# Attention, token mixing and a two-pass MLP on one core: plain products in the first pass, DVE adds the weights' words, input sums made ahead

## The chip, the core and the metric

The kernel runs on one core of a Trainium2 chip. The metric is the device time of one execution in microseconds (us); of several executions the median is given. TensorE is PE in the profile, VectorE DVE, ScalarE ACT, GpSimd POOL and SyncE, which issues the DMAs, SP.

## What is computed

```python
scores = scale * np.matmul(q, k.transpose(0, 1, 3, 2)) - np.log(S)      # B, H, S, D = 4, 12, 448, 64
x = (1.0 / (1.0 + np.exp(-scores))) @ v                                 # heads side by side: (4, 448, 768)
u = x + (x.transpose(0, 2, 1) @ U @ V).transpose(0, 2, 1)               # U, V of rank 32
x = u + np.maximum(u @ w_ch1, 0.0) @ w_ch2                              # 768 -> 3072 -> 768
theta = x @ w_theta
y = einsum('ts,bsd->btd', w_tok_r, x * cos(theta)) + einsum('ts,bsd->btd', w_tok_i, x * sin(theta))
u = x + y
out = u + np.maximum(u @ w_ch, 0.0)
```

The inputs q, k, v are float32; the weights arrive as float64, and the kernel puts their two 32-bit words together itself.

## The kernel before

After the attention the activations lie in SBUF, 768 channels as six strips of 128 partitions, two batches (896 columns) to a tensor: `XC` holds batches 0 and 1, a second tensor batches 2 and 3, which go to DRAM as `xb_d`. Every matmul of the MLP runs in float32 by three products: each operand is split in a high part (ScalarE copies it to the PE's type) and a low part (the rest, a subtraction on DVE, `lo_dve` L128, or on POOL, `lo_pool`, through L119).

**Two passes.** The MLP runs over batches 0 and 1 first and over 2 and 3 after that, each in `NB` = 12 blocks of 256 hidden columns; u = 0..11 is the first pass, u = 12..23 the second. Between them, in the turn, `XC` is swapped with `xb_d` through DRAM (L1123, L1124). A block has two stages. `ch1(u)` multiplies the activations with the block's w1 and applies ReLU; `ch2(u)` multiplies the result `g` with w2 in six parts of twelve matmuls each (L786 to L788), and after each part DVE adds the PSUM bank to `XC` (L790). There are two such banks (`ps_y`), so part m waits for the addition of part m - 2. A period is `ch1(u)` with `ch2(u - 1)`: part 0 of it ahead of `ch1`'s sixth step, parts 1 to 5 behind `ch1`.

**Plain or seven products.** A block's `ch1` is a 2x2 product of halves: two batches by two halves of hidden columns, each summed over two halves of the channels. `ch1_plain` makes it with 8 half products, 72 matmuls. `ch1_step` makes it with 7 (`STEPS`), 63 matmuls, from sums of weight blocks (S1 to S4, made in place by DVE in `w1_sums`, L277 to L280) and of inputs (T1, T2, T3 and a new B12, made by `t_chain` and `t_first`), and puts the four outputs together from PSUM banks and copies: `partial` (a copy `c` on ScalarE, L755), `whole` (DVE adds a bank to it, L759), `split_c` and `split_bank` (ReLU and split). Blocks below `PLAIN` = 2 are plain.

**Conversions.** In the first pass each period converts the weights of a later block, four tiles of 128x768: `Conv.size` loads the next tile and takes the Abs of the high words on ScalarE (L159), `sign` puts sign and mantissa together (DVE, L163 and L164), `low` scales the low words (DVE, L169 and L174), and `fin` in `keep` adds the two (POOL, L122) and stores the result in `w_d` in DRAM, from where the second pass loads it again. In the second pass the periods have two conversions each of what the last stage needs (`kept_jobs`: `tok0` to `tok6`, `wc0` to `wc5`, `th0` to `th5`); a `tok` tile is then transposed by PE (L356), and all of them go through one buffer, `sp`.

**What sets the order.** The order of every engine's instructions is written by hand: `period(u)` returns two hooks, `after_c(n)`, called behind the n-th step of `ch1`, and `after_y(m)`, called behind part m of `ch2`, and what they issue stands on its engine's queue at that place. `take` starts the next kept conversion with its Abs, `kstep` does its next step. At the turn, `turn_forms` swaps `XC`, loads and splits the inputs of the second pass and makes their sums.

Of the kernel before, what the change touches and what calls it, by code (L numbers as in the profile page):

```python
# [24 lines left out]
def tile_kernel(  # L25
# [551 lines left out]
    queue_w("w1", 2, 0)  # L577
    queue_w("w1", 2, 1)
    queue_w("w2", 1, 1)
    for u in range(2, NB):  # L580
# [289 lines left out]
    def part(t, d):  # L870
        return XC[:, d, t * S:(t + 1) * S]

    def chain(kk, los):
        return t_chain(kk, part(0, kk), part(1, kk), part(0, H3 + kk), part(1, H3 + kk), los)

    for t in range(2):
        for j in range(2):
            for h in range(2):
                ch1_plain(1, t, j, h)
            if (t, j) == (0, 0):  # L880
                w_jobs["w1", 2, 1].step()
                w_jobs["w1", 2, 0].step()
            if (t, j) == (0, 1):
                blocks(1, 0)
                plain_out(1, 0)
                w_jobs["w1", 2, 0].step()
                w_jobs["w1", 2, 0].step()
# [528 lines left out]
```

## Time and profile before

| | |
|---|---|
| median of 3 executions | 1378.13 us (1375.36 to 1379.81) |
| the profiled execution: its time, its span | 1383.18 us, 1381.4 us |
| granted PE clock over the span, as a share of 2.4 GHz | 0.934 |
| busy: PE, DVE, ACT, POOL | 1208.0, 876.0, 537.9, 574.2 us |

The span is what the profiler saw from the first to the last instruction; the execution's own time has what lies around it too. Busy times of the engines lie beside each other, so they don't add up to the span, and a share of it is an average over stages: attention up to about 200 us, the first pass up to about 676, the second up to about 1086, the last stage behind it. What bounds a stage is read from the stage's own window and from what PE waits for in it.

### The profile page before, as it was taken

What the parts mean: (1) busy time and instruction counts of PE and PEld (TensorE: products, weight loads), DVE (VectorE), ACT (ScalarE), POOL (GpSimd) and SP (SyncE); (2) the same over time, 40 slices, a digit from 0 to 9 for tenths busy, and PEclk for the clock granted to TensorE, in tenths of its full rate; (3) what the DMA queues carried; (4) which work ended last, traced back from release to release, by engine and by line L of the source; (5) the groups of instructions that cost most, each with busy time, mean ns of one, the idle gap of its engine ahead of it and who ended that gap; (6) DMA issues with size and microseconds to landing.
All of it is one profiled execution on the core that took longest, in us unless ns stands there. A gap on an engine that the chain in (4) does not pass through costs nothing.

```text
span 1381.4 us, 16213 instructions
## 1 busy us (share of the span) xinstructions
PE 1208.0 (87%) x6022; PEld 1016.9 (74%) x6022; DVE 876.0 (63%) x1061; ACT 537.9 (39%) x856; POOL 574.2 (42%) x399
## 2 busy tenths in 40 slices
PE   8899998487888887777587779989989999999998
PEld 4444457377777777676477778878879999999997
DVE  5677756688888898856445556677764464372443
ACT  6667762233333333322343334434434253261110
POOL 1121212366666666756344447755555042230000
PEclk9999999699888899999789999999999999999999
DMA  8677723144444334333542333444322600030244
GB/s 138 140 150 162 167 76 109 34 137 137 137 137 138 122 119 132 118 113 106 193 116 77 95 109 114 160 156 151 138 92 70 241 1 0 1 122 17 30 65 67
DMA packets 213279, 151.44 MB, mean 110 GB/s; under 512 B 160464, under 2 KB 194384, under 8 KB 213072
## 3 DMA queue, kind: packets, MB, share of 16 engines
q1 hardware_dynamic: 187216, 146.96, 36.1%
q10 hardware_dynamic: 25984, 3.44, 1.8%
q8 instruction: 47, 0.77, 0.2%
q14 instruction: 32, 0.26, 0.1%
HBM read 107.84 MB, written 42.53 MB: 109 GB/s over the span
## 4 chain that ended last, share of the span: by engine, by line
PE 44%; DVE 17%; issue 9%; POOL 9%; ACT 3%; DMA 1%; SPq 0%; POOLq 0%; DVEq 0%; ACTq 0%
PE ac L704 5%; PE y L786 5%; PE y L787 4%; PE y L788 4%; DVE ca_w L164 3%; POOL f_A L119 3%; PE y L1299 3%; PE y L1298 3%; PE y L1297 3%; PE bd L704 2%; DVE ws_w L163 2%; PE th L1221 2%; PE th L1224 2%; PE th L1222 2%; DVE XC L790 2%
## 5 line engine op out<-in xcount | busy, mean ns | idle before, releaser
L786 PE MATMUL y<-g,w 128*128 128x448 f32 x552 | 223.7, 405 | 121.9 <-DVE XC L790 121.8
L786 PEld LDWEIGHTS y<-g,w 128*128 128x128 f32 x552 | 114.7, 208 | 146.1 <-DVE XC L790 136.1
L790 DVE TENSOR_TENSOR XC<-y,XC 128x896 f32<-128x896 f32 x144 | 155.9, 1084 | 97.8 <-PE y L788 97.7
L787 PE MATMUL y<-g,w 128*128 128x448 f32 x552 | 217.3, 394 | 0.0
L788 PE MATMUL y<-g,w 128*128 128x448 f32 x552 | 216.0, 391 | 0.0
L122 POOL TENSOR_TENSOR ca_w<-ca_w,ws_w 128x768 f32<-128x768 f32 x48 | 93.9, 1956 | 170.2 <-DVE ws_w L174 160.6
L769 POOL TENSOR_TENSOR g<-c,g 128x448 fp32r<-128x448 f32 x66 | 89.6, 1361 | 98.3 <-ACT g L116 94.8
L788 PEld LDWEIGHTS y<-g,w 128*128 128x128 f32 x552 | 114.2, 207 | 10.8
L787 PEld LDWEIGHTS y<-g,w 128*128 128x128 f32 x552 | 115.0, 208 | 9.7
L491 ACT ACTIVATE A<-sc,bias_s 112x896 f32<-112x896 f32 x96 | 91.5, 1005 | 23.6 <-PE sc L487 23.5
L704 PE MATMUL ac<-u_T,f_S 128*128 128x448 f32 x396 | 90.2, 373 | 9.4 <-ACT c L755 9.4
L119 POOL TENSOR_TENSOR zl<-t,zh 128x768 fp32r<-128x768 f32 x23 | 42.7, 1880 | 129.5 <-ACT zh L116 129.5
L767 ACT ACTIVATE c<-c 128x448 f32<-128x448 f32 x66 | 37.7, 572 | 136.1 <-DVE c L759 136.1
L704 PEld LDWEIGHTS ac<-u_T,f_S 128*128 128x128 f32 x396 | 75.9, 192 | 16.7 <-ACT c L755 10.1
L755 ACT ACTIVATE c<-ac 128x448 f32<-128x448 f32 x66 | 35.9, 544 | 131.7 <-PE ac L704 126.0
L500 PE MATMUL av<-A,v 112*64 112x448 f32 x384 | 85.6, 569 | 1.0 <-ACT XO L116 1.0
L164 DVE SCALAR_TENSOR_TENSOR ca_w<-ca_w,ws_w 128x768 uint32<-128x768 uint32 x48 | 77.4, 1613 | 3.1
L119 POOL TENSOR_TENSOR f_S<-r,f_S 128x384 fp32r<-128x384 f32 x48 | 59.4, 1248 | 38.0 <-ACT f_S L116 37.9
L119 POOL TENSOR_TENSOR w<-ca_w,w 128x768 fp32r<-128x768 f32 x23 | 52.1, 2266 | 28.8 <-ACT w L116 26.6
L163 DVE TENSOR_SCALAR ws_w<-ws_w 128x768 uint32<-128x768 uint32 x48 | 60.7, 1264 | 4.4 <-POOL f L119 2.7
L1297 PE MATMUL y<-tok,zh 128*128 128x448 f32 x168 | 62.0, 369 | 0.0
L1298 PE MATMUL y<-tok,zh 128*128 128x448 f32 x168 | 61.7, 368 | 0.0
(225 smaller groups left out, 2699.7 us busy)
## 6 DMA issues: line engine op xcount, KB each, us to landing
ws_w<-in_moe_w_ch_dram SPq DMA_DIRECT2D x48, 768.0 KB, 5.0
w_d<-ca_w SPq DMA_DIRECT2D x48, 384.0 KB, 2.8
r<-w_d SPq DMA_DIRECT2D x24, 384.0 KB, 4.8
r<-w_d SPq DMA_DIRECT2D x12, 768.0 KB, 7.1
k<-in_k_dram SPq DMA_DIRECT2D x96, 56.0 KB, 2.9
q<-in_q_dram SPq DMA_DIRECT2D x92, 56.0 KB, 2.4
v<-in_v_dram SPq DMA_DIRECT2D x44, 112.0 KB, 2.9
ws_wc<-in_moe_w_ch_dram SPq DMA_DIRECT2D x6, 768.0 KB, 5.8
```

The lines of the kernel that those rows point to most:

```text
L119: nc.gpsimd.tensor_sub(o, a, b)
L122: nc.gpsimd.tensor_add(o, a, b)
L164: nc.vector.scalar_tensor_tensor(out=A, in0=A, scalar=3, in1=hw, op0=ALU.logical_shift_left, op1=ALU.bitwise_or)
L491: nc.scalar.activation(a, ps[:CP, :, :S], AF.Sigmoid, bias=bias_s[:CP], scale=SCALE)
L704: nc.tensor.matmul(o, l, r, start=first and kk == 0 and n == 0, stop=last and kk == H3 - 1 and n == 2, skip_group_check=more,)
L769: eng.tensor_sub(g[:, 1].bitcast(F32R), c, g[:, 0])
L786: nc.tensor.matmul(o, wh, gh, start=j == 0, stop=False)
L787: nc.tensor.matmul(o, wh, gl, start=False, stop=False)
L788: nc.tensor.matmul(o, wl, gh, start=False, stop=j == FB - 1)
L790: nc.vector.tensor_add(x, ps[:, :, :S], x)
L1297: nc.tensor.matmul(o, zh[:, sl], tok_h[:, i, :], start=n == 0, stop=False)
L1298: nc.tensor.matmul(o, zh[:, sl], tok_l[:, i, :], start=False, stop=False)
```

## The change

All twelve blocks of the first pass are plain (`PLAIN = NB`), with a hook of their own, `plain_period`; `period` serves the second pass alone. The addition of the two words goes from POOL to DVE: in the first pass from block 1 on (`adder`), and for `tok` and `wc` tiles. The T sums of the first pass go; those of the second pass are made during blocks 3 to 8 of the first (`sums_ahead`), from `xb_d`, with the new B12 kept in DRAM (`t4_d`), so that `turn_forms` only loads and splits. In the second pass the low parts of S1 to S4 go from POOL to DVE, and the steps of the kept conversions stand at other places.

```diff
-    wd_t, A_w = {}, {}
+    wd_t, A_w, adder = {}, {}, [nc.gpsimd]
...
         def fin(a, e):
-            add_pool(a, a, e)
+            adder[0].tensor_add(a, a, e)
...
     def conv_kept(name, src, kk, turns):
-            split(st["o"].bitcast(F32R), a, e, nc.vector if turns else nc.gpsimd)
+            split(st["o"].bitcast(F32R), a, e, nc.vector)
...
     def conv_tok(i):
-            add_pool(st["n"], a, e)
+            nc.vector.tensor_add(st["n"], a, e)
...
-    PLAIN = 2
+    PLAIN = NB
...
+    def sums_ahead(kk):
+        ts = [temp(f"ts{kk}_{n}") for n in range(3)]
+        b12, b22, b11 = ts
+        nc.sync.dma_start(out=b22, in_=xb_d[:, H3 + kk, S:])
+        nc.sync.dma_start(out=b12, in_=xb_d[:, kk, S:])
+        nc.sync.dma_start(out=b11, in_=xb_d[:, kk, :S])
+        def second():
+            nc.vector.tensor_sub(b22, b22, b12)
+            t_split("T3", kk, b22, lo_pool)
+            nc.vector.tensor_sub(b12, b12, b11)
+            t_split("T1", kk, b12, lo_pool)
+        def third():
+            nc.vector.tensor_add(b22, b22, b11)
+            t_split("T2", kk, b22, lo_pool)
+            b21 = temp(f"ts{kk}_3")
+            nc.sync.dma_start(out=b21, in_=xb_d[:, H3 + kk, :S])
+            ts.append(b21)
+        def fourth():
+            nc.vector.tensor_sub(ts[3], ts[3], b22)
+            nc.sync.dma_start(out=t4_d[:, kk], in_=ts[3])
+        return [second, third, fourth]
...
+    adder[0] = nc.vector
...
-    ends = [chain(kk, (lo_dve, lo_pool, lo_dve)) for kk in range(2)]
...
+    def plain_period(u):
+        a, b = (w_jobs["w1", u + 1, j] if more else None for j in range(2))
+        c, d = (w_jobs["w2", u, j] for j in range(2))
...
+        def after_c(n):
+            if n == 0:
+                if not more:
+                    load_w1(0)
+                step(a)
+                if two:
+                    w2_high(u - 1, 1, u - 1)
+                    w2_low(u - 1, 1, u - 1)
+                step(b)
...
+            if n == 7 and more:
+                for j in range(2):
+                    w1_plain(u + 1, j, u + 1, True)
...
+            if n == 7 and not more:
+                load_u(lo_in("B22"), xb_d[:, H3:, S:])
+                load_u(lo_in("B12"), t4_d)
...
+        def after_y(s):
...
+            if s == 1:
+                if more:
+                    w1_low(u + 1)
+                if two:
+                    step(d, 2)
+                    w2_high(u, 0, u)
+                    w2_low(u, 0, u)
...
+            if s == 3:
+                blocks(u, 1)
+                plain_out(u, 1)
+                if not more:
+                    w1_sums(0)
+                    w1_split(0, NB, "S3", "S2", "S1", "S4")
+                    w2_high(u, 1, u, True)
+                    w2_low(u, 1, u)
...
     def period(u):
         def after_c(n):
             if n == 0:
                 partial(u, 0, 0)
...
-                if second:
-                    take(kA)
+                kstep(kB)
+                kstep(kA)
...
         def after_y(s):
...
-                forms("S3")
-                kstep(kB)
...
+            if s == 2:
+                if nxt is not None:
+                    w1_sums(i + 1)
+                forms("S3", "S2", lo=lo_dve)
+            if s == 3:
+                forms("S1", "S4", lo=lo_dve)
...
+    for u in range(1, NB):
+        after_c, after_y = plain_period(u)
+        for n, (t, j, h) in enumerate(halves):
+            ch1_plain(u, t, j, h)
+            after_c(n)
+        ch2(u - 1, after_y)
...
     def turn_forms(s):
-        if s < 3:
-            t_chain(
+        if s == 0:
+            split_b("B22", lo_dve)
+            load_w1(1)
...
     kept_jobs[0].load()
+    take(kA)
     ch1(NB, after_c)
```

Three places of the engines' order follow. In the names, `y_4_1_1` is part 1 of block 4's `ch2` for batch 1, and `ws_w2_5_1` and `ca_w2_5_1` are the words of a conversion.

DVE in the first pass, before, while PE works on `ch2(4)` behind `ch1(5)`:

```order
L790 TENSOR_TENSOR XC_67<-y_4_1_1_3633,XC_67 128x2x448
L277 TENSOR_TENSOR ca_w1_6_1_3504<-ca_w1_6_1_3504 128x384
L278 TENSOR_TENSOR ca_w1_6_1_3504<-ca_w1_6_0_3488,ca_w1_6_1_3504 128x384
L279 TENSOR_TENSOR ca_w1_6_0_3488<-ca_w1_6_1_3504,ca_w1_6_0_3488 128x384
L280 TENSOR_TENSOR ca_w1_6_0_3488<-ca_w1_6_0_3488 128x384
L163 TENSOR_SCALAR ws_w2_5_1_3502<-ws_w2_5_1_3502 128x768
L164 SCALAR_TENSOR_TENSOR ca_w2_5_1_3609<-ca_w2_5_1_3609,ws_w2_5_1_3502 128x768
L790 TENSOR_TENSOR XC_67<-y_4_1_2_3655,XC_67 128x2x448
L169 TENSOR_SCALAR ws_w2_5_1_3502<-ca_w2_5_1_3609 128x768
L174 SCALAR_TENSOR_TENSOR ws_w2_5_1_3502<-ws_w2_5_1_3502 128x768
L790 TENSOR_TENSOR XC_67<-y_4_0_0_3676,XC_67 128x2x448
```

The same place in the change:

```order
L795 TENSOR_TENSOR XC_67<-y_4_0_0_3535,XC_67 128x2x448
L163 TENSOR_SCALAR ws_w2_5_1_3425<-ws_w2_5_1_3425 128x768
L164 SCALAR_TENSOR_TENSOR ca_w2_5_1_3501<-ca_w2_5_1_3501,ws_w2_5_1_3425 128x768
L795 TENSOR_TENSOR XC_67<-y_4_0_1_3551,XC_67 128x2x448
L169 TENSOR_SCALAR ws_w2_5_1_3425<-ca_w2_5_1_3501 128x768
L174 SCALAR_TENSOR_TENSOR ws_w2_5_1_3425<-ws_w2_5_1_3425 128x768
L216 TENSOR_TENSOR ca_w2_5_1_3501<-ca_w2_5_1_3501,ws_w2_5_1_3425 128x768
L795 TENSOR_TENSOR XC_67<-y_4_0_2_3576,XC_67 128x2x448
L795 TENSOR_TENSOR XC_67<-y_4_1_0_3596,XC_67 128x2x448
L718 SCALAR_TENSOR_TENSOR g_5_10_3610<-bc_5_3478,g_5_10_3610 128x448
```

The sums of weights ahead of the conversion are gone, the addition L216 stands behind L174, and all six additions to `XC` (now L795) are in this stretch and what follows it.

ScalarE at the turn, before:

```order
L116 ACTIVATE u_B22_2289<-u_B22_2289 128x1344
L116 ACTIVATE w2_12_1_5351<-r2_0_5105 128x768
L755 ACTIVATE c_12_00_5368<-ac_12_5358 128x448
L159 ACTIVATE ca_tok0_5372<-ws_tok0_5356 112x512
L755 ACTIVATE c_12_01_5395<-ac_12_5358 128x448
L755 ACTIVATE c_12_11_5421<-ac_12_5358 128x448
L767 ACTIVATE c_12_11_5421<-c_12_11_5421 128x448
```

In the change:

```order
L116 ACTIVATE u_B12_2289<-u_B12_2289 128x1344
L116 ACTIVATE w2_12_1_5173<-r2_0_4940 128x768
L159 ACTIVATE ca_tok0_5182<-ws_tok0_5178 112x512
L760 ACTIVATE c_12_00_5194<-ac_12_5184 128x448
L760 ACTIVATE c_12_01_5219<-ac_12_5184 128x448
L760 ACTIVATE c_12_11_5243<-ac_12_5184 128x448
L772 ACTIVATE c_12_11_5243<-c_12_11_5243 128x448
```

The Abs of `tok0` stood behind the first copy of `ch1(12)` and now stands ahead of it.

DVE in the second pass, during `ch2(13)`, before:

```order
L790 TENSOR_TENSOR XC_67<-y_13_1_1_5874,XC_67 128x2x448
L277 TENSOR_TENSOR r1_3_1_5749<-r1_3_1_5749 128x384
L278 TENSOR_TENSOR r1_3_1_5749<-r1_3_0_5747,r1_3_1_5749 128x384
L279 TENSOR_TENSOR r1_3_0_5747<-r1_3_1_5749,r1_3_0_5747 128x384
L280 TENSOR_TENSOR r1_3_0_5747<-r1_3_0_5747 128x384
L163 TENSOR_SCALAR ws_tok4_5754<-ws_tok4_5754 112x512
L164 SCALAR_TENSOR_TENSOR ca_tok4_5850<-ca_tok4_5850,ws_tok4_5754 112x512
L790 TENSOR_TENSOR XC_67<-y_13_1_2_5896,XC_67 128x2x448
L169 TENSOR_SCALAR ws_tok4_5754<-ca_tok4_5850 112x512
L174 SCALAR_TENSOR_TENSOR ws_tok4_5754<-ws_tok4_5754 112x512
L790 TENSOR_TENSOR XC_67<-y_13_0_0_5917,XC_67 128x2x448
L759 TENSOR_TENSOR c_14_01_5781<-bd_14_5758,c_14_01_5781 128x448
```

In the change:

```order
L795 TENSOR_TENSOR XC_67<-y_13_1_1_5699,XC_67 128x2x448
L795 TENSOR_TENSOR XC_67<-y_13_1_2_5714,XC_67 128x2x448
L284 TENSOR_TENSOR r1_3_1_5577<-r1_3_1_5577 128x384
L285 TENSOR_TENSOR r1_3_1_5577<-r1_3_0_5575,r1_3_1_5577 128x384
L286 TENSOR_TENSOR r1_3_0_5575<-r1_3_1_5577,r1_3_0_5575 128x384
L287 TENSOR_TENSOR r1_3_0_5575<-r1_3_0_5575 128x384
L128 TENSOR_TENSOR f_15_S3_5687<-r1_3_1_5577,f_15_S3_5687 128x384
L128 TENSOR_TENSOR f_15_S2_5688<-r1_3_0_5575,f_15_S2_5688 128x384
L795 TENSOR_TENSOR XC_67<-y_13_0_0_5736,XC_67 128x2x448
L128 TENSOR_TENSOR f_15_S1_5690<-r1_3_1_5577,f_15_S1_5690 128x384
L128 TENSOR_TENSOR f_15_S4_5691<-r1_3_0_5575,f_15_S4_5691 128x384
L764 TENSOR_TENSOR c_14_01_5605<-bd_14_5582,c_14_01_5605 128x448
```

Here the low parts of S1 to S4 (`f_15_S3` and the others) come in behind the sums, and the conversion's operations L163 to L174 that stood between the additions to `XC` are gone from this stretch.

## Rows read from the trace of the kernel before

**Rows 1.** The page, parts 1 and 2: busy time; 40 slices.

```profile
PE 1208.0 (87%) x6022; PEld 1016.9 (74%) x6022; DVE 876.0 (63%) x1061; ACT 537.9 (39%) x856; POOL 574.2 (42%) x399
...
PEclk9999999699888899999789999999999999999999
```

**Rows 2.** Waits of PE, 225 to 1071 us: waited for, us, times, longest.

```profile
PE y L786 <- DVE XC L790: 121.8, 29, 14.9
PE tkt L356 <- POOL sp_tok L122: 14.6, 3, 4.9
```

**Rows 3.** Windows by stage: length, busy us (x) by engine, clock, DMA, GB/s.

```profile
234.66:275.03 40.37, 19.45 (x74) 16.95 (x72) 26.66 (x38) 11.26 (x21) 12.43 (x11) 0.70 0.17 54
422.92:460.25 37.33, 30.89 (x137) 27.61 (x136) 30.74 (x30) 13.47 (x23) 25.06 (x18) 0.86 0.41 127
643.84:702.75 58.91, 38.29 (x137) 31.95 (x137) 27.46 (x32) 17.51 (x29) 21.07 (x17) 0.75 0.41 132
702.75:745.10 42.35, 33.06 (x144) 29.17 (x144) 22.35 (x28) 15.34 (x30) 24.28 (x21) 0.88 0.30 89
783.13:820.88 37.75, 30.79 (x145) 27.71 (x144) 20.30 (x24) 12.21 (x23) 18.09 (x14) 0.91 0.32 98
983.34:1016.12 32.78, 28.52 (x136) 25.04 (x135) 25.30 (x28) 14.56 (x26) 16.02 (x13) 1.00 0.32 121
1016.12:1043.48 27.36, 27.36 (x136) 25.35 (x135) 14.89 (x17) 11.15 (x21) 15.50 (x14) 1.00 0.31 116
```

**Rows 4.** Timeline of DVE: start, us, operation, idle before and releaser.

```profile
408.96 0.56 DVE L277 TENSOR_TENSOR ca_w<-ca_w 128x384 f32<-128x384 f32 x1 [3.36 <-POOL f_A L119]
...
414.17 1.08 DVE L790 TENSOR_TENSOR XC<-y,XC 128x896 f32<-128x896 f32 x1
```

**Rows 5.** Timeline of PE, at three of its waits.

```profile
415.30 0.74 PE L786 MATMUL y<-g,w 128*128 128x448 f32 x1 [6.91 <-DVE XC L790]
...
770.44 0.47 PE L786 MATMUL y<-g,w 128*128 128x448 f32 x1 [2.14 <-DVE XC L790]
...
778.00 1.01 PE L356 MATMUL tkt<-ident,sp_tok 112*128 112x112 f32 x4 [4.86 <-POOL sp_tok L122]
```

**Rows 6.** DVE and POOL by line, 422.92 to 460.25 us: busy, mean ns.

```profile
L164 DVE SCALAR_TENSOR_TENSOR ca_w<-ca_w,ws_w 128x768 uint32<-128x768 uint32 x4 | 6.8, 1710 | 0.3
L163 DVE TENSOR_SCALAR ws_w<-ws_w 128x768 uint32<-128x768 uint32 x4 | 6.6, 1645 | 0.0
...
L174 DVE SCALAR_TENSOR_TENSOR ws_w<-ws_w 128x768 f32<-128x768 uint32 x4 | 4.5, 1129 | 0.1
L169 DVE TENSOR_SCALAR ws_w<-ca_w 128x768 uint32<-128x768 uint32 x4 | 2.8, 704 | 0.0
...
L122 POOL TENSOR_TENSOR ca_w<-ca_w,ws_w 128x768 f32<-128x768 f32 x5 | 9.7, 1939 | 6.3 <-DVE ws_w L174 6.3
```

**Rows 7.** Lines of DVE over the whole run: count, duration ns shortest/median/longest.

```profile
L163 DVE TENSOR_SCALAR ws_w<-ws_w x48: 549/1359/2216, 19.1 to 629.7; 128x768 uint32<-128x768 uint32 x48
...
L164 DVE SCALAR_TENSOR_TENSOR ca_w<-ca_w,ws_w x48: 957/1634/2455, 19.7 to 631.1; 128x768 uint32<-128x768 uint32 x48
...
L169 DVE TENSOR_SCALAR ws_w<-ca_w x48: 543/556/2179, 23.5 to 633.7; 128x768 uint32<-128x768 uint32 x48
...
L174 DVE SCALAR_TENSOR_TENSOR ws_w<-ws_w x48: 958/960/2492, 24.1 to 634.9; 128x768 f32<-128x768 uint32 x48
...
L187 DVE TENSOR_TENSOR ca_th<-ca_th,sp_th x6: 958/1138/1326, 928.9 to 1016.8; 128x768 f32<-128x768 f32 x6
...
L790 DVE TENSOR_TENSOR XC<-y,XC x144: 1074/1082/1093, 253.5 to 1085.6; 128x896 f32<-128x896 f32 x144
```

**Rows 8.** Timelines of DVE, ScalarE and PE in the turn.

```profile
676.76 1.09 DVE L790 TENSOR_TENSOR XC<-y,XC 128x896 f32<-128x896 f32 x1 [1.26 <-PE y L788]
...
692.54 0.66 ACT L159 ACTIVATE ca_tok<-ws_tok 112x512 f32<-112x512 f32 x1 [13.12 <-DMA ws_tok<-in_moe_w_tok_r_dram]
...
693.68 3.73 PE L704 MATMUL ac<-u_T,f_S 128*128 128x448 f32 x9 [9.44 <-ACT c L755]
```

More of the change, by code (lines that the diff above doesn't have):

```diff
@@ L262, in w1_plain, with w1_low @@
             hi_act(t[:, 0], a)
-            lo_pool(t[:, 1], a, t[:, 0])
             w1_t[u, j, h] = t
+            if not later:
+                lo_pool(t[:, 1], a, t[:, 0])
+    def w1_low(u):
+        for j in range(2):
+            for h in range(2):
+                t = w1_t[u, j, h]
+                lo_pool(t[:, 1], w1_block(u, j, h), t[:, 0])
     USE = ("A11", "S3", "S2", "A12", "S1", "S4", "A22")
@@ L576, in tile_kernel @@
     queue_w("w1", 1, 1)
[L577 to L580, printed above, removed]
+    for u in range(1, NB):
         if u + 1 < NB:
@@ L866, in tile_kernel @@
         u_tile(uf2, n)
-    w_jobs["w1", 2, 0].step()
     late["sp"], sp_st = pool("sp")
[L870 to L887, printed above, removed]
-            if (t, j) == (1, 0):
-                w_jobs["w1", 2, 1].step()
-                w_jobs["w2", 1, 1].step()
-                ends = [chain(kk, (lo_dve, lo_pool, lo_dve)) for kk in range(2)]
-    for end in ends:
-        end()
-    chain(2, (lo_dve, lo_pool, lo_dve))()
-    for kk in range(H3):
-        t_first(kk, part(0, kk), part(1, kk), lo_pool if kk == 1 else lo_dve)
-    def y_first(s):
-        if s == 0:
-            w_jobs["w1", 2, 1].step()
-            w_jobs["w1", 2, 1].step()
-        if s == 1:
-            w1_forms(2)
-            w1_split(2, 2, "A11", "A12", "A22")
-        if s == 2:
-            w1_sums(2)
-            w1_split(2, 2, "S3", "S2", lo=lo_dve)
-            w_jobs["w2", 1, 1].step()
-        if s == 3:
-            blocks(1, 1)
-            plain_out(1, 1)
-            w1_split(2, 2, "S1")
-        if s == 4:
-            w1_split(2, 2, "S4")
-            w_jobs["w2", 1, 1].step()
-        if s == 5:
-            w_jobs["w2", 1, 1].step()
-            w_jobs["w1", 3, 0].step()
-    ch2(0, y_first)
     kq = list(kept_jobs)
@@ L946, in period, with forms @@
+    ahead = []
+    def period(u):
+        i = u % NB
         lone, last = u == NB, u == NU - 1
-        def step(j):
-            if j is not None:
-                j.step()
-        def forms(*names):
+        nxt = None if last else u + 1
+        def forms(*names, lo=lo_pool):
             if nxt is not None:
-                w1_split((i + 1) % NB, nxt, *names)
+                w1_split(i + 1, nxt, *names, lo=lo)
         def after_c(n):
@@ L1056, in after_y @@
                 kstep(kB)
-                kstep(kB)
-                if not second and i + 2 < NB:
-                    w_jobs["w1", i + 2, 0].step()
+                if u < NU - 2:
+                    take(kA)
                 if u == NU - 2:
                     load_w2(i + 1)
-                if i == NB - 1 and not last:
-                    w2_high(i, 1, u, True)
-                    w2_low(i, 1, u)
         return after_c, after_y
@@ L1129, in tile_kernel @@
     kept_jobs[0].load()
+    take(kA)
     ch1(NB, after_c)
```

184 lines of the change are left out of this document (84 added, 100 removed).

## The prediction

> **What bounds the kernel now.** I read the page first. TensorE (PE) is busy for 1208 of 1381.4 us, and its granted clock stands at 0.8 or 0.9 over much of the middle of the span and at 0.6 in one slice [rows 1]: PE is the bound only where it doesn't wait. So the next view is PE's waits in the two passes. Two entries hold nearly all of them: 121.8 us in 29 waits for VectorE's (DVE's) `XC` addition of L790, which frees one of the two `y` banks, and 14.6 us in three waits for GpSimd's (POOL's) addition in a `tok` conversion, L122 [rows 2].
>
> The windows by stage say what each is worth [rows 3]. The last of them is the measure: 27.36 us for 135 matmuls (the row counts one of a neighbour) with PE busy throughout, at the full 2.4 GHz (granted clock 1.00), so 0.2027 us for each. A first-pass period of the same 135 matmuls takes 37.33 us, with DVE busy for 30.74, POOL for 25.06 and a clock of 0.86. Those ten microseconds over the floor are what the change is about.
>
> The timelines show how such a wait arises. The sums of the next block (L277) wait 3.36 us for POOL, which has the conversion's addition ahead of their operands; the conversion queued behind the sums follows, and only then the `XC` addition, 5.2 us after L277 began [rows 4]. Meanwhile PE stands for 6.91 us. Its first matmul after this takes 0.74 us, the first after a wait of 2.14 us only 0.47 [rows 5], and the granted clock of windows with long waits is 0.70 to 0.88 [rows 3]. A short wait costs itself; a long one costs the half clock (1.2 GHz) after it too.
>
> POOL also slows DVE. In that window the four operations of a conversion take 1.645, 1.710, 0.704 and 1.129 us [rows 6], 5.19 together; at their shortest they take 0.549, 0.957, 0.543 and 0.958, 3.01 together [rows 7]. Four conversions thus lose 8.7 us beside 25.06 us of POOL work: 0.35 us per us of POOL.
>
> **The change, part by part.** All against the profiled execution of 1383.18 us, which is 5.05 us (0.4%) over the median of the three runs.
>
> 1. `ch2(0)`, 234.66 to 275.03, takes 40.37 us with PE busy for 19.45 [rows 3]. DVE makes the T sums and the first sums of weights there; both go. What is left is 72 matmuls, 72 x 0.2027 = 14.6, and half a microsecond of waits: 15.1. **Minus 25.3.** Ends: 14.6 and, with one wait of the size in [rows 5] for the conversions in it, 22.
>
> 2. Ten periods of the first pass, 275.03 to 643.84, 368.8 us [rows 3]. Plain blocks have 72 products' matmuls instead of 63, so the floor rises from 27.36 to 144 x 0.2027 = 29.19 us: 18.3 us are paid in ten periods. Against this DVE and POOL lose their chain: no sums, no `c` partials, and the conversion's addition runs on DVE right behind the operation that feeds it. DVE's load without POOL beside it is four conversions of 3.01 plus an addition of 0.96 (DVE's L187, 128x768, at its shortest [rows 7]), 15.9; six `XC` additions of 1.08, 6.5; four ReLU differences, estimated at 0.6 by their 448 columns, 2.4; in six periods the sums made ahead, some 1.2. That is 24.8 to 26.0. The POOL work left beside it is four low parts of half a block, estimated at half of a 1.94 us operation [rows 6] each, two of about 2.0 and one or two for the T forms, 8 to 10 us; at 0.35 it adds 3.2. DVE then needs 28 to 29.2 us, PE 29.2. Two engines so nearly equal, with two `y` banks between them, don't meet without waits: the additions of parts 3 to 5 stand behind the fourth conversion, as the order listing of DVE shows. I take 2 us of waits per period, short ones that keep the full clock: 31.2. The lower end is 29.3 (no waits), the upper 35.1 (each microsecond of POOL delays DVE by a whole one, 26 + 9). The last period has no conversion for a next block: 29.6. Together 9 x 31.2 + 29.6 = 310.4. **Minus 58.4.** The loads that the sums made ahead issue on SP's queue (four per strip, plus a store) are hidden as long as they are issued a part before their use; without that cover DVE would wait for each, some microseconds in six periods, which the upper end holds.
>
> 3. The turn, 643.84 to 702.75, 58.91 us [rows 3]. `ch2(11)` becomes 14.6 of matmuls and some 5 of waiting for the last weights' low parts, which POOL makes behind four others: 19.6. What follows it doesn't go: the swap of `XC` with DRAM and the load of `ws_tok` behind it in SP's queue. From the last `XC` addition (676.76) to the Abs of `tok0` (692.54) it takes 15.8 us, and PE waits 9.44 of them [rows 8]. The change puts this Abs ahead of `partial(12,0,0)` on ScalarE (the order listing shows it), so PE stops after two products where it had done four. After the Abs (0.66) and the copy (0.5) five products of nine matmuls remain, 9.1, and the half clock after such a wait costs about 3.6 (the three products after it took 9.07 us to 702.75, 5.5 at full clock). 19.6 + 0.3 + 15.8 + 1.2 + 9.1 + 3.6 = 49.6. **Minus 9.3.** Ends: minus 15 and nothing.
>
> 4. Second pass, `ch1(13)` to `ch1(22)`, 702.75 to 1016.12, nine periods in 313.4 us [rows 3]. Its matmuls stay, 9 x 27.36 = 246.2. The `tok` addition goes to DVE, behind its own source, so the 4.86 us before each of three transposes [rows 2, 5] go; four low parts per period move from POOL to DVE behind the sums that they read. I add the six transposes (1.0 us each, [rows 5]) and remaining waits. A `tok` period now has 10.4 us over the floor, of which 4.9 is the wait and 2 the transposes; of the other 3.5 I leave 1.5. Of the 5.4 of a `th` period (983.34) I leave 2.0, of a `wc` period, which has neither, 1.2. Three periods of each: 14.1; and 4 for the first, which starts at a low clock. 246.2 + 6 + 14.1 + 4 = 270.3. **Minus 43.1.** Ends: minus 25 and minus 55.
>
> What lies before 234.66 and after 1043.48 keeps its work; I count nothing. The sum is minus 25.3, 58.4, 9.3 and 43.1, or 136.1: 1247.1 for that execution, and less 5.05 **1242 us** on the median's scale.
>
> [...] The same window shows the operations of two SBUF inputs and those of one grow beside POOL, while `XC` additions, whose one input is in PSUM, take 1.074 to 1.093 us in all 144 cases [rows 7]. [...]
>
> **The rivals.**
> A. DVE is the bound of the first pass: 35.1 per period. For it: the adds have two SBUF inputs, and L174 has been as long as 2.49 us [rows 7]. Against: 0.35. It costs 9 x 3.9 = 35: 1277.
> B. The second pass gains nothing, since its waits are replaced: DVE gets the low parts and the `tok` additions ahead of its `XC` additions (the order listing of DVE in `ch2(13)`). Against: DVE was busy for 20.3 of 37.75 us there, POOL for 18.1 [rows 3]. 1242 + 43 = 1285.
> C. Slower: every conversion runs at its longest, 2.22 + 2.46 + 2.18 + 2.49 and 1.33 for the addition [rows 7], 10.7. Four take 43, and with the 10 of additions and ReLU a period takes 53. The mechanism is DVE's queue in the first pass alone, and it decides from 31.2 + 136/9 = 46.3 us per period on; at 47 the time is 1242 + 142 = 1384. Against it stand the medians, far nearer the shortest.
> D. PE is never kept waiting: 29.3 per period (17 less), and the second pass at its lower end (12 less): 1213.
> That the change doesn't do what it says is excluded by the order listings.
>
> **How the numbers follow.** Forecast 0.68, A 0.14, B 0.09, C 0.05, D 0.04. The predicted time is the forecast's, 1242. The range from 1210 to 1290 takes in D, A and B and the ends of the terms 3 and 4; A and B together, and C, lie outside. A measurement of this kernel tells 0.3% (4 us) from no change. Only C, and little else, ends above 1378: faster 0.95, the same 0.01, slower 0.04.
>
> **What would show it.** Right: PE's windows between starts of `ch1` of 29.3 to 33 us in the first pass with 144 matmuls and a clock near 1.00; a wait of PE for `XC` additions under 40 us in all; no wait of transposes for POOL; 15 us for `ch2(0)`; a wait of about 13 us in the turn for ScalarE's copy behind `ca_tok`. Wrong: conversions' operations on DVE still above 4.5 us per four (A), second-pass periods near 35 us (B), first-pass DVE busy throughout at over 35 us (A, C).

## The result, and the profile after

The changed kernel takes 1292.88 us (median of 4 runs, 1290.99 to 1295.45) against 1377.41 us before: a ratio of 0.939, 95% interval 0.936 to 0.941, or 84.5 us less. Forecast were 1242 us with a range from 1210 to 1290, so the direction was right and the size was not: the time lies 51 us above the forecast and 3 us outside its range.

The profiled execution took 1295.45 us (span 1293.7). The page answers to [rows 1] so:

```profile
PE 1198.7 (93%) x6112; PEld 1010.9 (78%) x6112; DVE 870.8 (67%) x1102; ACT 483.5 (37%) x752; POOL 328.7 (25%) x232
...
PEclk9989999999999999987899999989999999999999
```

POOL lost 245 us of work, DVE almost none, and PE's granted clock is 0.971 over the span and lowest around the turn (0.77 in the turn's window). PE's waits from 190 to 1000 us, as in [rows 2] (waited for: us in total, times, longest):

```profile
PE ac L709 <- ACT c L760: 34.2, 12, 15.8
PE y L791 <- DVE XC L795: 23.5, 31, 1.7
PE tkt L363 <- DVE XC L795: 8.3, 3, 2.8
PE bd L709 <- DVE c L764: 5.1, 1, 5.1
PE y L793 <- POOL f_w L119: 3.7, 1, 3.7
```

The wait for `XC` additions fell from 121.8 to 23.5 us, as forecast. Now the first entry is PE's wait for ScalarE's copy `c`: 34.2 us. Before, it was 11.1, nearly all of it the wait in the turn that the prediction names (in the window of [rows 2]):

```profile
PE ac L704 <- ACT c L755: 11.1, 4, 9.4
```

Of the 34.2 us, 15.8 are that wait in the turn, and most of the rest lies in the second pass, which had 1.5 us of such waits before. Where, the windows by stage tell; they answer to [rows 3] in this order: `ch2(0)`, two periods of the first pass, the turn, and four of the second pass (the first, a `tok`, a `wc` and a `th` period).

```profile
235.60:250.26 14.66, 14.66 (x73) 13.45 (x72) 10.06 (x12) 2.29 (x4) 0.68 (x1) 1.00 0.36 118
281.37:312.78 31.41, 29.80 (x145) 26.88 (x144) 29.35 (x32) 8.22 (x14) 9.71 (x6) 1.00 0.53 169
312.78:345.43 32.65, 30.46 (x145) 26.80 (x144) 30.77 (x33) 10.89 (x18) 13.59 (x9) 1.00 0.43 132
569.00:621.74 52.74, 32.60 (x138) 28.72 (x136) 17.81 (x18) 9.91 (x15) 11.02 (x9) 0.77 0.43 137
621.74:661.61 39.87, 31.62 (x145) 27.97 (x144) 26.69 (x39) 15.43 (x30) 12.45 (x11) 0.91 0.28 88
695.11:728.94 33.83, 30.69 (x146) 27.20 (x145) 21.89 (x31) 12.34 (x23) 10.62 (x9) 0.95 0.33 112
758.72:789.00 30.28, 28.62 (x136) 24.98 (x135) 24.68 (x31) 13.09 (x23) 10.40 (x9) 1.00 0.43 157
891.00:927.81 36.81, 31.14 (x138) 27.56 (x136) 27.68 (x33) 14.54 (x25) 10.54 (x9) 0.91 0.29 108
```

Against the forecast, from starts of the stages:

| stage | before | forecast | after | miss |
|---|---|---|---|---|
| `ch2(0)` | 40.4 | 15.1 | 14.7 | -0.4 |
| first pass, ten periods | 368.8 | 310.4 | 318.7 | +8.3 |
| turn | 58.9 | 49.6 | 52.7 | +3.1 |
| second pass, nine periods | 313.4 | 270.3 | 306.1 | +35.8 |

The rest is 1.5 us around them. So the miss lies in the second pass: its old waits went, and it gained 7 us where 43 were counted. In a `tok` period the transposes no longer wait 4.9 us for POOL but 2.7 to 2.8 for a `y` bank. In a `th` period, 32.8 to 34.0 us before, PE now waits 4.5 us for ScalarE's copy. This is the timeline of ScalarE and PE there (start, us, operation, idle before and releaser):

```profile
866.31 0.84 ACT L181 ACTIVATE ca_th<-ca_th 128x768 f32<-128x768 f32 x1 [6.44 <-DVE ws_th L178]
867.06 0.53 ACT L760 ACTIVATE c<-ac 128x448 f32<-128x448 f32 x1
...
867.64 3.73 PE L709 MATMUL ac<-u_T,f_S 128*128 128x448 f32 x9 [4.54 <-ACT c L760]
```

The copy stands behind L181, the scaling of a `th` tile, which waits for DVE. Its nine matmuls then take 3.73 us instead of 1.99; the granted clock is 0.50 from 867.64 to 871.37. And this is the timeline of DVE and POOL late in `ch2` of a `tok` period:

```profile
653.42 1.02 DVE L128 TENSOR_TENSOR f_S<-r,f_S 128x384 fp32r<-128x384 f32 x2
654.35 1.08 DVE L795 TENSOR_TENSOR XC<-y,XC 128x896 f32<-128x896 f32 x1
655.36 3.43 DVE L128 TENSOR_TENSOR f_S<-r,f_S 128x384 fp32r<-128x384 f32 x2
...
655.11 1.84 POOL L119 TENSOR_TENSOR w<-r,w 128x768 fp32r<-128x768 f32 x1 [5.91 <-ACT w L116]
656.90 1.47 POOL L774 TENSOR_TENSOR g<-c,g 128x448 fp32r<-128x448 f32 x1
```

The low parts of S3 and S2 take 1.02 us together, those of S1 and S4 take 3.43, and POOL is at work for all but the last 0.4 us of these. It is so in every period of the second pass (3.43 to 3.44 us for the pair, ten times from 655 to 957 us), and whatever stands behind them on DVE starts that much later.

### The profile page after: what moved, and what is told of

Its sections match the earlier page's. It is cut to its first block, busy times and chain, and to the rows that moved or that the text cites. A ratio compares the mean times of both kernels' runs of the same rounds, so it can differ in the third digit from the quotient of the medians.

```text
span 1293.7 us, 16034 instructions
## 1 busy us (share of the span) xinstructions
PE 1198.7 (93%) x6112; PEld 1010.9 (78%) x6112; DVE 870.8 (67%) x1102; ACT 483.5 (37%) x752; POOL 328.7 (25%) x232
## 3 DMA queue, kind: packets, MB, share of 16 engines
q10 hardware_dynamic: 25984, 3.44, 1.9%
## 4 chain that ended last, share of the span: by engine, by line
PE 39%; DVE 10%; issue 5%; ACT 1%; POOL 1%; DMA 1%; DVEq 0%; ACTq 0%; SPq 0%; POOLq 0%
PE ac L709 5%; DVE f_S L128 3%; PE y L791 3%; PE y L793 3%; PE y L792 3%; PE y L1304 3%; PE y L1303 3%; PE y L1305 3%; PE bd L709 3%; PE th L1227 2%; PE th L1230 2%; PE th L1228 2%; PE wc L1384 2%; PE wc L1385 2%; PE wc L1386 2%
## 5 line engine op out<-in xcount | busy, mean ns | idle before, releaser
L791 PE MATMUL y<-g,w 128*128 128x448 f32 x552 | 207.5, 376 | 23.7 <-DVE XC L795 23.5
L795 DVE TENSOR_TENSOR XC<-y,XC 128x896 f32<-128x896 f32 x144 | 155.0, 1086 | 79.1 <-PE y L793 78.9
L792 PE MATMUL y<-g,w 128*128 128x448 f32 x552 | 203.3, 368 | 0.0
L793 PE MATMUL y<-g,w 128*128 128x448 f32 x552 | 203.2, 368 | 0.0
L791 PEld LDWEIGHTS y<-g,w 128*128 128x128 f32 x552 | 104.8, 190 | 44.6 <-DVE XC L795 34.1
L793 PEld LDWEIGHTS y<-g,w 128*128 128x128 f32 x552 | 104.6, 189 | 9.1
L792 PEld LDWEIGHTS y<-g,w 128*128 128x128 f32 x552 | 104.9, 190 | 8.4
L119 POOL TENSOR_TENSOR f<-ca_w,f 128x384 fp32r<-128x384 f32 x48 | 63.7, 1355 | 133.8 <-ACT f L116 133.8
L774 POOL TENSOR_TENSOR g<-c,g 128x448 fp32r<-128x448 f32 x36 | 44.7, 1242 | 176.0 <-ACT g L116 176.0
L709 PE MATMUL ac<-u_T,f_S 128*128 128x448 f32 x216 | 55.8, 409 | 32.7 <-ACT c L760 32.7
L709 PEld LDWEIGHTS ac<-u_T,f_S 128*128 128x128 f32 x216 | 45.3, 214 | 40.4 <-ACT c L760 36.4
L119 POOL TENSOR_TENSOR w<-r,w 128x768 fp32r<-128x768 f32 x23 | 42.9, 1870 | 89.8 <-ACT w L116 71.9
L1305 PE MATMUL y<-tok,zl 128*128 128x448 f32 x168 | 61.7, 367 | 0.0
L159 ACT ACTIVATE ca_w<-ws_w 128x768 f32<-128x768 f32 x48 | 43.1, 909 | 48.4 <-DMA ws_w<-in_moe_w_ch_dram 44.2
L1227 PE MATMUL th<-th_r,xh 128*128 128x384 f32 x168 | 57.3, 341 | 0.1
```

Of the source, the lines that this page charges most:

```text
L119: nc.gpsimd.tensor_sub(o, a, b)
L709: nc.tensor.matmul(o, l, r, start=first and kk == 0 and n == 0, stop=last and kk == H3 - 1 and n == 2, skip_group_check=more,)
L791: nc.tensor.matmul(o, wh, gh, start=j == 0, stop=False)
L792: nc.tensor.matmul(o, wh, gl, start=False, stop=False)
L793: nc.tensor.matmul(o, wl, gh, start=False, stop=j == FB - 1)
L795: nc.vector.tensor_add(x, ps[:, :, :S], x)
```

## The experiments

Three theories were to be told apart. **Queue order**: three waits (L181 ahead of the copy, the transposes' bank, `tok0`'s load behind the swap) each hold PE by themselves. **DVE beside POOL**: DVE's operations that read two SBUF tensors are stretched by POOL's, and DVE is late because of it. **DVE's load**: DVE simply has too much to do. Medians are compared with the 1292.88 us above. Over the profiles `ch1(0)` begins anywhere from 189.8 to 194.7 us, through the attention alone, and what follows the start of `ch1(23)`, the last stage above all, takes from 335.2 to 339.0 us. So differences of a few us are read from windows, not from the medians.

**1. `e1_th_scale_later`**

```diff
 def low(self):
-    nc.scalar.activation(A, A, AF.Copy, scale=INV_HI)
 def fin(a, e):
+    if turns:
+        nc.scalar.activation(a, a, AF.Copy, scale=INV_HI)
```

> The scaling of a th tile on ScalarE (L181) is issued one step later, behind the copy partial(u,0,1). Theory: in the three th periods PE waits 4.5 us each for that copy, which stands on ScalarE's queue behind L181, which waits for DVE; the half clock behind the wait costs 2.4 us more. Both go: the three periods of 35.5, 36.3 and 36.8 us fall to about 29.5, some 20 us together, 1273 us. Rival (DVE is the bound of these periods, busy 27.5 of 36 us): the wait comes back as one for XC additions, the periods stay over 33 us and the time above 1286 us.

1286.57 us. The waits of 4.5 us went, but the `th` periods take 35.0, 33.5 and 33.4 us, not 29.5; this is one of them:

```profile
851.15:884.60 33.45, 28.52 (x137) 24.97 (x135) 27.11 (x33) 14.64 (x25) 11.11 (x9) 1.00 0.42 142
```

The clock is back at 1.00; PE's waits are now 1.6 to 2.0 us for copies further on, behind the next steps of the same conversion. The theory of the queue held for the wait and not for its worth: 6 of 20 us. The time and the periods are those that the rival named, but its wait, for `XC` additions, didn't come. ScalarE's queue shows the same order one copy further on: in the period shown the scaling waits 4.05 us for DVE ahead of the next copy, and PE waits 1.62 us for that copy.

**2. `e2_tkt_own_bank`**

```diff
-    ps = ps_y.tile([P, 2, 512], F32, tag="y", name=f"tkt_{i}", bufs=2)
+    ps = ps_g.tile([P, 512], F32, tag="ad", name=f"tkt_{i}", bufs=1)
```

> The transposes of a tok tile write the PSUM bank ad, which the second pass does not use, instead of a y bank. Theory: the three waits of 2.7 us of a transpose for an XC addition are for the bank alone; they go, and the slower clock behind each (1.4 us) too: 12 us in all, 1280 us, tok periods of 33.5 to 33.8 us fall to about 29.5. Rival (DVE is late in these periods, the bank only shows it): PE waits as long at the next part of ch2, less than 4 us gained, 1289 us or more.

1285.37 us; the second to fourth period of the stage take 31.0, 32.5 and 28.2 us for 33.5, 33.8 and 29.8. PE's wait moved from the bank to the transposes' source:

```profile
PE tkt L363 <- DVE sp_tok L358: 5.3, 3, 1.8
```

So DVE is late, as the rival says, and the bank was only half of it.

**3. `e3_tok0_load_early`**

```diff
+    kept_jobs[0].load()
     ch2(NB - 1, turn_forms)
     after_c, _ = period(NB)
-    kept_jobs[0].load()
     take(kA)
```

> The load of tok0's words is issued before ch2(11) and the swap of XC on SP's queue, instead of behind it. Theory: the wait of 15.8 us in the turn (ScalarE's copy behind the Abs of tok0, which waits for this load behind the swap) goes whole, with some 3 us of half clock behind it: 19 us, 1274 us. Rival (the swap itself or the forms of the second pass are late as well): a wait of 8 us or more remains in ch1(12) or ch1(13), at most 10 us gained, 1283 us or more.

1272.12 us: 20.8 us gained by the medians, and 18.0 in `ch1(12)` itself, which took 32.12 us in the changed kernel. It has one wait of 0.6 us for ScalarE left:

```profile
584.65:598.78 14.13, 13.50 (x69) 12.05 (x67) 5.81 (x9) 4.46 (x9) 2.31 (x3) 1.00 0.73 247
```

**4. `e4_three`** is these three edits together.

> The three edits together. Theory: the three waits lie in different stretches and add up: 20 + 12 + 19 = 51 us, 1242 us. Rival (DVE bounds the second pass whatever the queues): less than 25 us together, 1268 us or more.

1260.05 us (0.915 of before, 0.912 to 0.918), 32.8 us gained: what the three gave singly (6.3 + 7.5 + 20.8 = 34.6) adds up, but 13 us of it are in the nine periods of the second pass, where 32 were expected.

**5. `e12_s_lows_only`**: the changed kernel with

```diff
-                forms("S3", "S2", lo=lo_dve)
+                forms("S3", "S2", lo=lo_pool)
...
-                forms("S1", "S4", lo=lo_dve)
+                forms("S1", "S4", lo=lo_pool)
```

> The changed kernel with one edit: the low parts of S1 to S4 in the second pass run on POOL, as before. Theory: that these four subtractions run on DVE just when POOL makes the low part of w2 is the main reason why the second pass gained so little; without it DVE is on time, the transposes find their bank free, and tok periods fall from 33.7 to about 30 us, wc periods by 1 us, th periods by 1.5 (their wait for ScalarE's copy behind L181 stays): some 18 us, 1275 us. Rival (the bank and the order of ScalarE's queue make the waits by themselves): less than 8 us, 1285 us or more.

1269.60 us, 23.3 us gained by undoing this one piece. Second pass (a `tok`, a `wc`, a `th` period):

```profile
685.63:713.80 28.17, 28.17 (x146) 26.07 (x145) 21.38 (x27) 12.22 (x23) 15.59 (x13) 1.00 0.41 135
...
741.25:770.12 28.87, 27.92 (x137) 25.20 (x136) 22.64 (x26) 13.06 (x24) 15.73 (x13) 1.00 0.47 165
...
798.99:834.48 35.49, 30.27 (x137) 27.50 (x136) 25.60 (x28) 14.56 (x26) 15.75 (x14) 0.90 0.39 134
```

From `ch1(14)` on, `tok` periods have PE busy for their whole 28.17 us though the transposes still take a `y` bank: their bank comes free in time. The `th` periods keep their wait. `ch1(13)` to `ch1(22)` takes 280.5 us for 306.1.

**6. `e9_w_low_later`**: `e4_three` with

```diff
 if s == 3:
-    w2_high(i, 0, u)
-    w2_low(i, 0, u)
...
 if s == 5:
+    w2_high(i, 0, u)
+    w2_low(i, 0, u)
```

> The three edits of e4_three with the low parts of S1 to S4 left on DVE, and the split of w2 (ScalarE's copy, POOL's low part) issued behind part 5 of ch2 instead of behind part 3, so that POOL doesn't work on it beside S1 and S4. Theory (DVE is held up by POOL, not by the work itself): the two subtractions fall from 3.43 us to 2 us or less, since only POOL's g subtraction is left beside them, and the time falls by 8 us or more, 1252 us or less. Rival (DVE simply has too much work): the periods stay within 0.5 us of those of e4_three, 1257 us or more.

1255.79 us, by the medians 4 us less than `e4_three`: between the two. The nine periods from `ch1(13)` to `ch1(22)` take 285.5 us for 292.9, 7.4 less, which is near the theory's 8. The timeline of DVE shows why:

```profile
784.05 1.97 DVE L128 TENSOR_TENSOR f_S<-r,f_S 128x384 fp32r<-128x384 f32 x2
...
789.87 2.49 DVE L188 TENSOR_TENSOR sp_wc<-ca_wc,ws_wc 128x768 fp32r<-128x768 f32 x1
```

The subtractions fell from 3.43 to 1.97 us, with DVE's work unchanged, so it is POOL's operation that had held them. It is so in every period: the low part of S1 takes 0.55 us for 2.00, and that of S4, which still lies beside POOL's `g`, stays at 1.51. The same low part of w2 then held L188, 0.96 us in `e4_three` and 2.49 here. The cost moves with POOL's operation.

**7. `e8_s_lows_pool`**: `e4_three` with the edit of 5.

> The three edits of e4_three, and the low parts of S1 to S4 in the second pass on POOL again instead of DVE. Theory: two of these operations take 3.43 us on DVE beside POOL's low part of w2 and 1.02 us without it; on POOL they leave DVE 4.4 us per period, its additions to XC and its conversions start earlier, and the periods of 33.5 and 30.2 us fall by 2 us or more: 20 us, 1240 us. Rival (POOL is late then): PE waits for POOL's f_S at the second step of ch1, nothing gained or slower, 1260 us or more.

1241.22 us (0.902 of before). A `tok` and a `th` period:

```profile
637.71:665.88 28.17, 28.17 (x146) 26.06 (x145) 21.41 (x27) 12.24 (x23) 15.61 (x13) 1.00 0.37 122
...
843.21:877.23 34.02, 30.59 (x136) 27.31 (x135) 24.66 (x28) 14.52 (x26) 16.41 (x13) 0.90 0.31 117
```

The theory's number, and no wait of PE for POOL came in the second pass. Against run 4 the `tok` periods fell by 2.8 to 4.9 us, the `wc` periods by only 0.8 to 1.5, and the `th` periods by 3.0 and 1.6, but for the last, which took 34.0 for 33.4.

**8. `e5_before_dve_add`**: the kernel before with

```diff
 def fin(a, e):
-    add_pool(a, a, e)
+    nc.vector.tensor_add(a, a, e)
```

> The kernel before with one edit: every addition of a weight's two words runs on DVE. Theory: the addition on POOL is one link of the first pass's chain (DVE waits 3.4 us for POOL ahead of the sums), so the period falls by some 2.5 us from 36.9, to 34.4: 1353 us. Rival (the sums and copies of the seven products make the waits, not the addition): less than 1 us per period, 1368 us or more. Second rival (DVE is already the fuller engine and the 3.8 us more per period delay the XC additions): slower than 1376 us.

1338.43 us, for 1376.09 of the kernel before measured beside it (a ratio of 0.973): 37.7 us from one line. The nine periods from `ch1(2)` to `ch1(11)` take 298.2 us for 332.7; PE's long waits for `XC` in them, 6.4 to 7.0 us each, fell to 2.8 to 3.9.

**9. `e6_after_pool_add`**: the changed kernel without

```diff
-    adder[0] = nc.vector
```

> The changed kernel with the additions of the first pass back on POOL. Theory: with plain blocks nothing waits for the addition within the period, so DVE loses 3.8 us of its own work and gains some 2.7 us of delay beside POOL; the periods stay within 1 us of 31.9 and the time within 10 us of 1293. Rival (the addition on DVE is what makes the first pass fast): periods of 34 us or more, 1315 us or more.

1286.19 us: not slower. The nine periods from `ch1(2)` to `ch1(11)` take 283.3 us for 286.9. Periods 3 and 4:

```profile
277.27:307.37 30.10, 29.93 (x145) 26.95 (x144) 25.61 (x26) 7.68 (x13) 16.66 (x10) 1.00 0.52 154
307.37:341.59 34.22, 30.08 (x146) 26.80 (x145) 31.65 (x30) 11.20 (x19) 20.66 (x13) 1.00 0.47 147
```

With plain blocks the addition is better on POOL in period 3 and most others (30.0 to 30.2 us for 31.1 to 31.4) and worse in periods 4, 6 and 8, in which the second half of each strip's sums is made (34.1 to 34.4 for 32.7 to 33.5). These are waits of DVE around period 4, with the addition on POOL (300 to 345 us):

```profile
DVE ts L824 <- DMA ts<-xb_d: 1.6, 1, 1.6
DVE ts L826 <- DMA ts<-xb_d: 1.0, 1, 1.0
```

Without the additions DVE stands at the first sums of a strip for the loads of their inputs, 2.6 to 3.5 us at the start of each of these three periods; in the changed kernel it waits there for at most 0.8. It is the wait that the prediction names for loads that are not issued early enough. The line that gave 37.7 us alone gives nothing beside the plain blocks: both break the same chain.

**10. `e7_no_pool_lows`**

```diff
-    lo_pool(t[:, 1], w1_block(u, j, h), t[:, 0])
+    hi_act(t[:, 1], w1_block(u, j, h))
...
-            lo_pool(o, a, h)
+            hi_act(o, a)
```

The second of these edits is for the w2 splits of the first pass alone.

> The changed kernel without POOL work beside the conversions of the first pass: the low parts of w1 and w2 (blocks 2 to 11, but for the halves of the last w2) are left out and a copy on ScalarE is put in their place, so that the computation is changed. Theory: POOL delays DVE by 0.35 us per us, 3 us of DVE's time per period; DVE's busy time falls from about 29 to 26 us, PE's waits of 0.7 to 1.5 us at parts 4 and 5 go, and the periods fall from 31.2 to 29.6 and from 33 to 31: some 17 us, 1276 us. Rival (the waits come from the order, XC additions behind a conversion's operations): DVE's busy time falls as well but the periods stay over 30.7, 1287 us or more.

1267.16 us, 25.7 us gained by the medians; the nine periods take 264.7 us for 286.9, 22.1 less. The same period as the second row of windows above:

```profile
274.49:303.85 29.36, 29.36 (x146) 26.96 (x144) 25.21 (x32) 11.39 (x20) 0.00 (x0) 1.00 0.58 180
```

With POOL idle PE has no wait at all in this period, and DVE is busy for 25.21 us, not 29.35. POOL's 9.71 us had cost DVE 4.14: 0.43 us per us. By line, in the changed kernel (busy us, mean ns):

```profile
L795 DVE TENSOR_TENSOR XC<-y,XC 128x896 f32<-128x896 f32 x6 | 6.4, 1084 | 2.1 <-PE y L793 2.1
L164 DVE SCALAR_TENSOR_TENSOR ca_w<-ca_w,ws_w 128x768 uint32<-128x768 uint32 x4 | 5.0, 1240 | 0.7 <-issue 0.4
L216 DVE TENSOR_TENSOR ca_w<-ca_w,ws_w 128x768 f32<-128x768 f32 x4 | 4.5, 1134 | 0.1
```

and with POOL idle:

```profile
L798 DVE TENSOR_TENSOR XC<-y,XC 128x896 f32<-128x896 f32 x6 | 6.5, 1090 | 4.0 <-PE y L796 4.0
L216 DVE TENSOR_TENSOR ca_w<-ca_w,ws_w 128x768 f32<-128x768 f32 x4 | 3.8, 960 | 0.1
...
L164 DVE SCALAR_TENSOR_TENSOR ca_w<-ca_w,ws_w 128x768 uint32<-128x768 uint32 x4 | 3.8, 958 | 0.1
```

The conversions' operations take their shortest times, also those with a single input, which lies in SBUF (L163 and L169: 0.83 and 0.76 us in the changed kernel, 0.56 each with POOL idle); the `XC` additions are the same either way.

**11. `e10_all`** adds three edits to `e8_s_lows_pool`:

```diff
+        adder[0] = nc.vector if u in (4, 6, 8) else nc.gpsimd
...
+                    w2_high(u, 1, u, True)
+                    w2_low(u, 1, u)
                     w1_sums(0)
                     w1_split(0, NB, "S3", "S2", "S1", "S4")
-                    w2_high(u, 1, u, True)
-                    w2_low(u, 1, u)
...
-                nc.scalar.activation(a, a, AF.Copy, scale=INV_HI)
...
+                nc.vector.tensor_scalar(out=A, in0=A, scalar1=INV_HI, scalar2=None, op0=ALU.mult)
```

> e8_s_lows_pool with three more edits: the first pass's additions on POOL but in periods 4, 6 and 8, which have the sums made ahead (7 periods of 31.2 us go to 30.1: 8 us); the halves of the last w2 split ahead of the sums for block 12, so that ch2(11) doesn't wait 3.7 us for POOL (5 us with the half clock); the scaling of a th tile on DVE instead of ScalarE, so that no step goes from DVE to ScalarE and back within it (2.5 us in each of three periods). Theory: they add up to 20 us, 1221 us. Rival (the additions on POOL shift DVE's operations onto its low parts, and DVE's 1 us more per th tile makes XC late): less than 8 us, 1233 us or more.

1236.03 us: by the medians 5 of 20. But `ch1(0)` begins 4.8 us earlier in this profile than in that of `e8_s_lows_pool`, and from there to the start of `ch1(22)` only 1.3 us are gained. The periods with the addition on POOL take 30.0 to 30.4 us as expected, but periods 4, 6 and 8 take 35.6 to 36.0, more than with either engine alone:

```profile
304.73:340.76 36.03, 32.19 (x146) 29.30 (x145) 31.71 (x34) 11.24 (x19) 13.18 (x9) 0.91 0.44 140
```

In it PE waits 3.8 us for `XC` once, and the granted clock of the period is 0.91. The wait for POOL's last w2 went from the turn. The `th` periods gained nothing: 32.7 to 33.1 us, for 31.8 to 34.0 in run 7. ScalarE and PE in one of them:

```profile
817.35 0.84 ACT L116 ACTIVATE sp_th<-ca_th 128x768 fp32r<-128x768 f32 x1 [5.74 <-DVE ca_th L181]
818.10 0.89 ACT L159 ACTIVATE ca_th<-ws_th 128x768 f32<-128x768 f32 x1
818.89 0.52 ACT L760 ACTIVATE c<-ac 128x448 f32<-128x448 f32 x1
...
819.47 2.12 PE L709 MATMUL ac<-u_B,f_S 128*128 128x448 f32 x9 [2.42 <-ACT c L760]
```

The scaling runs on DVE now, but the copy `c` stands behind the next operation of the same conversion, L116, which waits for DVE in its turn.

**12. `e11_pool_add`** drops the first of these edits and `adder[0] = nc.vector` too.

> e10_all with all additions of the first pass on POOL, also in periods 4, 6 and 8. Theory: switching the engine between periods is what made those three take 36 us (POOL's backlog meets DVE's additions); with POOL throughout they take 34.2 as in e6_after_pool_add, and the time falls by 5 us, 1231 us. Rival (the three edits of the turn and of th shift the first pass): no gain, 1235 us or more.

1235.72 us (0.899 of before, 0.896 to 0.901), by the median no faster than `e10_all`. The first pass gained more than was expected: its nine periods take 279.6 us for 288.3, with this one in place of the 36 us:

```profile
309.00:341.82 32.82, 29.98 (x145) 26.75 (x144) 31.07 (x30) 11.31 (x19) 21.07 (x13) 1.00 0.48 154
```

In its profile `ch1(0)` begins 3.4 us later than in that of `e10_all`, and what follows the start of `ch1(23)`, the same in both kernels, takes 3.5 us longer, which hides most of that. The three periods take 32.8 to 33.6 us here and 34.1 to 34.4 in run 9, with the same order in the first pass: DVE stands for the loads for 1.9 to 2.7 us, so their landing differs from profile to profile. Run 11 had 2.1 to 3.7 us of these waits; they don't account for all of its 36 us, and what else the switch between engines costs was not taken apart.

**13. `e13_t_lows_dve`**: `e11_pool_add` with

```diff
-            t_split("T3", kk, b22, lo_pool)
+            t_split("T3", kk, b22, lo_dve)
```

and T1 and T2 likewise.

> e11_pool_add with the low parts of the sums made ahead (T1, T2, T3, blocks 3 to 8) on DVE instead of POOL. Theory (POOL's work beside DVE is what costs): POOL has 3.4 us less in two periods, DVE 1.8 us more of its own; periods 4, 6 and 8 fall from 34.2 to 33 us or less, 1227 us. Rival (DVE is full in these periods, every operation put on it counts): periods of 34.2 us or more, 1231 us or more.

1242.91 us, 7 us slower. The same period:

```profile
308.53:344.37 35.84, 30.24 (x146) 26.73 (x145) 33.18 (x33) 11.28 (x19) 17.58 (x10) 1.00 0.45 141
```

POOL has 3.5 us less, DVE 2.1 more, and the period is 3 us longer; DVE also waits 1.9 us for ScalarE's high parts ahead of these subtractions. In these periods what is put on DVE's queue decides, as the rival says: here taking work from POOL doesn't pay if it is put on DVE.

## Why the prediction was wrong, and where it was right

**Right.** PE's waits for `XC` additions bound the first pass; they fell under the 40 us that were named. `ch2(0)` came out at 14.7 us. Six of the nine like periods took 31.1 to 31.4 us for 31.2, with PE at a granted clock of 1.00; the waits are the short ones at parts 4 and 5. The price of POOL, 0.35 us per us, measured 0.43 (run 10), which leaves rival A where it was: no period took 35 us. The wait in the turn came as described (15.8 us; about 13 were named), and run 3 shows that the load behind the swap was all of it. The half clock behind long waits came too: from 200 to 1080 us in the changed kernel the granted clock is 0.50 in the first us behind each of PE's waits of 3.2 to 15.8 us and 1.00 behind those of 1.3 to 1.7 us; behind the transposes' waits of 2.7 to 2.8 us it is 0.55 to 0.88 in the first us and 0.50 in the next two. The profile gives the clock as a share, and 1.2 GHz stands as an estimate: before, at 0.50, matmuls of 448 columns follow each other every 0.374 us (415.83 to 421.06 us), 1.2 columns per ns, of which 2.4 is the double; at 1.00 they follow every 0.2027 us, 2.2 columns per ns.

**Wrong: part 4, the second pass**, 35.8 of the 48 us between forecast and profiled execution. Two sentences of it failed.

"four low parts per period move from POOL to DVE behind the sums that they read" was given no cost in the sum; the only reason that the prediction has for this is the one against rival B, DVE's spare time in that stage. What counts is what POOL does at that moment. Two of the four lie beside POOL's low part of w2 and its `g`, and were held for 2.4 us out of 3.3 us of POOL's work, right ahead of the last `XC` additions and of everything that DVE owes ScalarE and PE at the start of the next period. The 0.35 of the first pass was used for the sum of part 2 and not here. Run 5 undoes this piece alone: 25.6 of the 35.8 us come back in this stage. Run 6 shows that the meeting counts by itself: 7.4 us come back with DVE's load unchanged. Run 7 takes 19.6 us off run 4 in the same stage; how much of the rest is DVE's load and how much the meetings that run 6 left or moved, no run separates.

"Of the 5.4 of a `th` period (983.34) I leave 2.0" looked at the waits before and not at what the reordered steps put ahead of each other on ScalarE: L181, which waits for DVE, ahead of the copy that PE waits for. The listings that the prediction used showed DVE there, not ScalarE. With S1 to S4 back on POOL the `th` periods still take 34.9 to 35.5 us (run 5), 105.2 together where 88.1 were counted. Moving L181 one step on puts it ahead of the next copy (runs 1 and 7), and moving it to DVE leaves L116 in its place (run 11): none of the runs takes the conversion's steps out from ahead of the copies. The three periods of run 11, 32.7 to 33.1 us, have 12 us of PE's waits in them, 6.9 for ScalarE's copy `c`; what an order without these would give was not run.

Rival B had the mechanism, a replaced wait with DVE's low parts ahead of its `XC` additions, and its 1285 us is the nearest of the times given; but its chance was put at 0.09, and the stage did gain 7 us where the rival has none, so its nearness is in part luck. What spoke against it, that DVE was busy for only 20 of 38 us, is an average over the period, and the wait is a matter of its end.

**Mis-sized: part 2**, 8.3 us. Periods 4, 6 and 8 took 32.7 to 33.5 us, and the last one 31.9 for 29.6, with one wait of PE of 1.7 us for `XC`: it has no conversions for a next block but the sums and splits for the second pass, which part 2 left out. In period 4 DVE was busy for 30.8 us where 28 to 29.2 were counted, and POOL for 13.6 where 8 to 10 were. **Part 3**, 3.1 us: 1.0 lies in `ch2(11)`, where 5 us were counted for the wait for POOL's last w2, which took 3.7, and nothing for the half clock behind it (granted clock 0.83 in this stretch); run 11 shows that the wait goes when the split is issued first. The other 2.1 lie in `ch1(12)`: from the last `XC` addition (589.82 us) to the Abs of `tok0` (608.11) it took 18.3 us where the 15.8 of before were counted.

**The gain itself** was put down to the right parts but not separably. The addition on DVE gives 37.7 us in the kernel before (run 8) and costs 3.5 us over nine periods in the kernel after (run 9): the chain from POOL's addition over the sums to the `XC` addition breaks by either cut.

Where operations meet, the trace tells more than the average does. These are the two subtractions of the pair, one by one:

```profile
655.36 2.00 DVE L128 TENSOR_TENSOR f_S<-r,f_S 128x384 fp32r<-128x384 f32 x1
...
657.28 1.50 DVE L128 TENSOR_TENSOR f_S<-r,f_S 128x384 fp32r<-128x384 f32 x1
```

The first ends 0.4 us behind POOL's first operation (656.95 us) and the second 0.4 us behind POOL's second (658.37); in all ten cases the pair ends 0.41 or 0.42 us behind POOL's second operation. Apart from POOL each takes 0.55 us. What in POOL's operations holds them, no run shows. `XC` additions, with one input in PSUM, stay at 1.07 to 1.09 us in all 144 cases, beside POOL or not. The averages of 0.35 and 0.43 are taken over a whole period of the first pass; here 2.4 us were lost beside 3.3 us of POOL's work, 0.73 us per us.
